# Spreading the preparation of operands over more steps of a two-MLP attention kernel

## The chip, the cores and the metric

The kernel runs on one core of a Trainium2 chip. The metric is device time in microseconds (us): the median of three runs before the change is 1218.3 (1217.76 to 1219.68).

## The reference

Attention runs twice per batch and head: 32 packed queries attend to 576 keys, and then the 576 queries attend to the 32 packed results. Its output, 4608 tokens of 512 features, goes through a first MLP (512 to 2048 to 512, squared ReLU) and a second one (512 to 1024 to 512, with a softmax gate and a layer norm between its two products):

```python
p_packed = sm_attn(p, k, v)                 # B=8, H=8, S=576, D=64, 32 packed rows
x = sm_attn(q, p_packed, p_packed)          # -> [4608, 512]
h = np.maximum(x @ w_in, 0.0)               # first MLP
y = h * h @ w_out
h = y @ w_in2                               # second MLP
solu = h * softmax(h)
ln = (solu - mean(solu)) / np.sqrt(var(solu) + 1e-06) * g_ln
out = ln @ w_out2
```

All of it is float32. A product is made of three TensorE products of rounded parts: each operand x is held as a high half (x rounded to the type fp32r) and a low half (x minus the high half), and high times high, high times low and low times high are added.

## The kernel before, in words

**Steps.** The first MLP runs as 256 steps (variable `i` in the loop at the end of `build`): eight batches, two halves of 288 tokens, 16 slices of 128 hidden features. In step i, `h1` issues six matmuls into a PSUM bank (the names h, ah, al, slot), ScalarE writes the ReLU (rg), ScalarE or GpSimd by turns the square, ScalarE the high half of the square and VectorE the low half (both in the tile ghl); the low half has its place in VectorE's order after the work listed for step i + 1 (`lows`). `ymm`, called three steps later (LAG), issues twelve matmuls of ghl with the weights woh and wol into four accumulators Y. After 16 slices Y is copied out, two copies by ScalarE and two by VectorE, into ys, which goes to y_d in DRAM; the accumulators are used again by the next Y product. These copies come with steps 162, 178, 194, 210, 226 and 242. The start of a step is taken below as the start of ScalarE's ReLU, which is its first operation.

**Work beside the steps.** `at_step(i, fn)` puts a function on step i's list, and it runs when the loop comes to that step. From step 138 (`R0`) to 245 the program order of VectorE, ScalarE and GpSimd is the order written by these lists (`strict`); SyncE's DMAs, and the matmuls of `mm`, are always in that order. Elsewhere a planner orders the instructions by their expected times. On these lists stand the second attention of batches 5 to 7 (`s2_jobs`: that of batch 6 spreads over steps 163 to 185, of batch 7 over 195 to 217), the loads of the first-layer operands (`load_slot`), and the two preparations that the change is about:

- `decode_at` (line 521): 16 units of the second MLP's weights, one every `PD` = 5 steps from step 138. A unit loads 512 KB (raw), and four to six steps later ScalarE and VectorE turn its 64-bit floats into 32-bit ones (dw): one ScalarE operation, one shift and two other operations on VectorE. The first eight units belong to the first weight, the others to the second. After units 3 and 7, and after units 9, 11, 13 and 15, `quads` (line 635) combines four blocks into the seven operands of Strassen's scheme over the next six steps: seven high halves by ScalarE, seven low halves (op) and four differences (dw) by VectorE, each operand stored to wi_d or wx_d.
- `pre_y` (line 753): 14 pairs of 128-token blocks of y, one every `RD` = 6 steps from step 138. A pair loads 512 KB (yf) and makes seven operands of it in steps 4 to 8 after the load: ScalarE writes the high halves, GpSimd the differences and five low halves, VectorE two low halves (yo). Each operand is stored to yc_d two steps after it is made, from one of seven buffers.

**Into the second MLP.** At step `t0` = 230 the memory of both preparations is given up and the pools w2 and y01 take its place. The operands of the first two pairs (`fetch_y`, seven loads of 256 KB each) are loaded at steps 234 and 240, the 14 operand tiles of the first weight (`load_wi`, 512 KB each) at steps 231 to 244, one a step, in the order of the list `WO`; those of the second weight (`load_wx`, 28 of 256 KB) at steps 244 to 257, two a step, into the tiles of the first MLP's second weight as its last products free them. `h2(0)`, the first product of the second MLP for one pair (seven Strassen products of six matmuls), its softmax and layer norm stand at step 249. After the loop come 18 rounds of `h2`, the transposes `tr` and the last product `ou`, ordered by the planner.

`strassen` (line 830) uses its right-hand operands in this order:

```python
p1 = prod("11", "11"); prod("12", "21"); prod("S2", "T2"); prod("S3", "T3")
prod("S1", "T1"); prod("S4", "22"); prod("22", "T4")
```

Of the kernel before, what the change touches and what calls it, by code (L numbers as in the profile page):

```python
# [27 lines left out]
NPRE = 14  # L28
# [4 lines left out]
def f(ap):  # L33
    return ap.bitcast(F32)


def build(tc, qT, kT, vP, pT, w_in, w_out, w_in2, w_out2, g_ln, out):
# [25 lines left out]
    def dma(out, in_):  # L63
        pin(SP.dma_start(out=out, in_=in_))
# [19 lines left out]
    def bank(name):  # L84
        return ps.tile([P, 512], F32, tag="a", name=name, bufs=4)
# [432 lines left out]
    def at_step(i, fn):  # L518
        jobs.setdefault(i if i == "first" else T0 + i, []).append(fn)

    def decode_at(i, mk):
        d = {}
        at_step(i, lambda: d.setdefault("u", mk()))
        for j in range(3):
            at_step(i + 4 + j, lambda: d["u"].step())
# [24 lines left out]
    for b in range(2, B):  # L550
# [9 lines left out]
        for s in range(8):  # L560
            i = 16 + 2 * s + 3
            if b == 2:
                i = (17, 19, 21, 23, 25, 31, 33, 35)[s]
            if b == 4:
                i = max(i, 9 + 24 * s // 5)
# [25 lines left out]
    def load_wi(i):  # L591
        k, o = divmod(i, 7)
        t = W2["p"].tile([P, 2, 512], F32R, name=f"wi{k}{WO[o]}")
        dma(f(t.rearrange("p a c -> p (a c)")), wi_d[k, o])
        wi.setdefault(k, {})[WO[o]] = t
# [7 lines left out]
    WO = ("11", "T1", "22", "21", "T3", "T2", "T4")  # L603
# [9 lines left out]
    def wi_unit(k, q):  # L613
        r0, c0 = (k + 2 * (q // 2)) * P, (q % 2) * 1024

        def fin(wf):
            wq[q] = wf[:, 0]
            if q == 3:
                quads(wi_d[k], 512, *(wq[i] for i in range(4)))

        return Decode(W2["d"], w_in2[r0:r0 + P, c0:c0 + 1024], (1, 512), fin, bufs=(2, 1, 6))

    def wx_unit(k, half):
        q = k + 4 * half

        def fin(wf):
            A.activation(wf[:, 0], wf[:, 0], AF.Copy, scale=W2["g"][:, q:q + 1])
            for i in range(2):
                wq[2 * half + i] = wf[:, 0, i * 256:(i + 1) * 256]
            if half:  # L630
                quads(wx_d[k], 256, *(wq[i] for i in range(4)))

        return Decode(W2["d"], w_out2[q * P:(q + 1) * P], (1, 512), fin, bufs=(2, 1, 6))
# [54 lines left out]
    for n in range(8):  # L688
        i = P1 + 1 + PS * n
# [7 lines left out]
        unit_at(P2 + 1 + u * 12 // 5, 1, u // 2, u % 2, lambda: X["p"], (3, 2, 2))  # L697
    p1 = P2 + 1 + 36 + 9
    at_step(p1, open_prep)
    PD = 5  # L700
    for u in range(16):
        mk = (lambda u=u: wi_unit(u // 4, u % 4)) if u < 8 else (lambda u=u: wx_unit((u - 8) // 2, u % 2))
        decode_at(p1 + 1 + PD * u, mk)
    t0 = 230
    assert p1 + 1 + PD * 15 + 6 <= t0
    at_step(t0, lambda: W2["dst"].close())
    at_step(t0, lambda: X["yst"].close())
# [9 lines left out]
    def halves(t):  # L717
        return [t[:, x * 256:(x + 1) * 256].rearrange("p (a c) -> p a c", a=2) for x in range(2)]


    def operands(q, put, eng):
        a11, a12, a21, a22 = q["11"], q["12"], q["21"], q["22"]
        los = []

        def comb(out, x, y, op=ALU.subtract):
            eng("c").tensor_tensor(out=out, in0=x, in1=y, op=op)

        def split(n, x):
            hi, lo, done = put(n)
            A.copy(hi, x)  # L730

            def go():
                eng(n).tensor_tensor(out=lo, in0=x, in1=f(hi), op=ALU.subtract)  # L733
                done()
            los.append(go)

        def low():
            for fn in los:
                fn()
            los.clear()  # L740

        return [[(split, "11", a11), (split, "12", a12), (split, "22", a22), (comb, a21, a21, a22, ALU.add)], [(low,)],
                [(split, "S1", a21), (comb, a11, a21, a11), (comb, a12, a12, a11), (comb, a22, a22, a11)],
                [(low,), (split, "S2", a11), (split, "S4", a12), (split, "S3", a22)], [(low,)]]

    def quadrants(yl, yr):
        return {"11": yl[:, :, :P], "12": yr[:, :, :P], "21": yl[:, :, P:], "22": yr[:, :, P:]}


    R0, RD = 138, 6  # L750
    assert R0 + RD * (NPRE - 1) >= 213 > R0 + 5 * RD >= 101

    def pre_y(m):
        i0 = R0 + RD * m
# [36 lines left out]
    def places(i):  # L791
        c = {}
        for j, n in enumerate(AO):
            if i < 2:
                if i == 0 and j < 4:
                    t = atp.tile([P, S], F32R, tag=f"a{'hl'[j % 2]}{j // 2}", name="y0", bufs=2)[:, :512]
                else:
                    t = W2["y"].tile([P, 512], F32R, name=f"y{i}{n}")
            elif j < 4:
                if j % 2 == 0:  # L800
                    u = big4(1, [P, 2, 512], "y2", F32R)
                t = u[:, j % 2]
            else:
                t = t25("1" if j == 4 else "2", "y2", F32R)[:, :512]
            c[n] = t
        return c

    def fetch_y(i):
        m = ORDER[i]
        c = places(i)  # L810
        if m < NPRE:
            for j, n in enumerate(AO):
                dma(f(c[n]), yc_d[m][:, j])
            ytl[i] = {n: halves(t) for n, t in c.items()}
            return
        ytl[i] = {n: halves(t) for n, t in c.items()}
        y2 = [p2.tile([P, 2, 256], F32, tag=f"yf{k}", name="yf", bufs=1) for k in range(2)]
        for k in range(2):
            dma(y2[k], y_d[:, 2 * k:2 * k + 2, m * 256:(m + 1) * 256])
        for js in operands(quadrants(*y2), lambda n: (*ytl[i][n], lambda: None), lambda n: V if n in ("22", "12") else G):  # L820
            for fn, *x in js:
                fn(*x)
# [34 lines left out]
    def h2(m):  # L857
        c = ytl.pop(m)
        if m == 0:
            e = big.tile([P, 2, 512], F32, tag="big", name="e", bufs=4)  # L860
        t = [big.tile([P, 2, 512], F32, tag="big", name="hs", bufs=4) for _ in range(2)]
        mx = {}

        def fin(i, o, x, y):
            n = W2["p"].tile([P, 1], F32, tag=f"mx{i}", name="mx", bufs=2)
            V.tensor_tensor_reduce(out=o, in0=x, in1=y, scale=1.0, scalar=mx.get(i, -3.4028234663852886e38), op0=ALU.add, op1=ALU.max,  # L866
                                   accum_out=n)
            mx[i] = n

        strassen(lambda l, k: (c[l][0][:, k], c[l][1][:, k]), wi, 2, 512, (lambda: bank("h")) if m == 0 else (lambda: psh.tile([P, 512], F32, tag="h", name="h", bufs=3)),  # L870
                 t[0][:, 0], t[0][:, 1], t[1][:, 0], t[1][:, 1], vadd, fin)
        hs[m] = t
        for i, h in enumerate(t):
            nm = W2["p"].tile([P, 1], F32, tag="nm", name="nm2", bufs=2)
            V.tensor_scalar_mul(nm, mx[i], -1.0)
            if m:
                e = p2.tile([P, 2, 512], F32, tag="e", name="e", bufs=1)
            sm = W2["p"].tile([P, 1], F32, tag="sm", name="sm3", bufs=2)
            A.activation(e, h, AF.Exp, bias=nm, accum_out=sm)  # L879
            V.tensor_scalar_add(sm, sm, 1e-9)  # L880
            V.reciprocal(sm, sm)
            V.scalar_tensor_tensor(out=h, in0=e, scalar=sm, in1=h, op0=ALU.mult, op1=ALU.mult)  # L882
            st = W2["p"].tile([P, 2, 6], F32, tag="st", name="st", bufs=1)
            for n in range(2):
                V.bn_stats(out=st[:, n, :], in_=h[:, n, :])  # L885
            mv = W2["p"].tile([P, 2], F32, tag="mv", name="mv", bufs=2)
            V.bn_aggr(out=mv, in_=st)
            rstd = W2["p"].tile([P, 1], F32, tag="rstd", name="rstd", bufs=2)
            V.tensor_scalar_add(rstd, mv[:, 1:2], 1e-6)
            G.tensor_tensor(out=rstd, in0=rstd, in1=mhalf, op=ALU.pow)  # L890
            if next(TURN["LNA"]) == "V":
                V.tensor_scalar(out=h, in0=h, scalar1=mv[:, 0:1], scalar2=rstd, op0=ALU.subtract, op1=ALU.mult)  # L892
            else:
                nb = W2["p"].tile([P, 1], F32, tag="nb", name="nb", bufs=1)
                V.scalar_tensor_tensor(out=nb, in0=mv[:, 0:1], scalar=-1.0, in1=rstd, op0=ALU.mult, op1=ALU.mult)
                A.activation(h, h, AF.Identity, bias=nb, scale=rstd)  # L896
# [2 lines left out]
        W2["yst"].close()  # L899

    for i in range(2):
        at_step(t0 + 4 + 6 * i, lambda i=i: fetch_y(i))
    for i in range(14):
        at_step(t0 + 1 + i, lambda i=i: load_wi(i))
    at_step(249, lambda: h2(0))


    K0 = Pack(0, era, False)
# [23 lines left out]
    for t in range(max(max(j for j in jobs if j != "first"), T0 + N + LAG - 1) + 2):  # L932
        i = t - T0
# [196 lines left out]
```

## Time and profile before

| what | us |
|---|---|
| median of three runs | 1218.3 |
| the profiled execution | 1216.89 |
| its span, first to last instruction | 1215.1 |
| TensorE matmuls busy | 1148.2 (94%) |
| VectorE busy | 879.2 (72%) |
| ScalarE busy | 665.6 (55%) |
| GpSimd busy | 581.8 (48%) |

The mean granted TensorE clock is 0.983 of full speed. In the rows below, L58 and L53 are helpers (`mm` and `Engine`) through which most instructions are issued, so instructions are told apart by their tiles: `Y<-ghl,woh` is a Y product, `op<-dw` a combination of weights, `yo<-yf` an operand of y. PE is TensorE, DVE VectorE, ACT ScalarE, POOL GpSimd, SP SyncE. What stands in square brackets behind an instruction is the idle time of its engine just before it, and what ended that.

### The profile page before, as it was taken

The numbers are of one execution on the slowest core, as the hardware profiler recorded it, in microseconds if no ns is written. First come the engines' busy times: TensorE is split into PE (matmuls) and PEld (weight loads), VectorE is DVE, ScalarE is ACT, GpSimd is POOL, SyncE is SP. The second block draws the span as 40 slices with busy tenths as digits, with TensorE's granted clock in tenths as the row PEclk, the third lists the DMA queues.
The fourth block names the chain that finished last, engine by engine and source line by source line (L and its number), as shares of the span: only waits on it lengthen the run. The fifth ranks groups of instructions, "written<-read, shape, count | busy, mean of one in ns | idle before, by whom it ended". The sixth has DMA issues, their size and how long they took to land. (4 is left out here: it accounts for less than half of the span.)

```text
span 1215.1 us, 24017 instructions
## 1 busy us (share of the span) xinstructions
PE 1148.2 (94%) x8652; PEld 1055.3 (87%) x8652; DVE 879.2 (72%) x1700; ACT 665.6 (55%) x1505; POOL 581.8 (48%) x591
## 2 busy tenths in 40 slices
PE   6678899999999999999998899999999999999998
PEld 3368899898999998998998899998889899889897
DVE  4787588745326766579877982257989789889886
ACT  3476555344445555566666674435554655655553
POOL 1112254534225544487866781113654764745743
PEclk9988899999999999999999999999999999999999
DMA  9667697655155899789699799653142143223201
GB/s 331 217 198 193 187 300 225 227 203 199 57 198 155 214 290 303 203 308 378 228 393 340 255 368 366 223 171 114 44 144 90 38 143 105 87 83 109 79 23 48
DMA packets 124775, 238.04 MB, mean 196 GB/s; under 512 B 16624, under 2 KB 44272, under 8 KB 124656
## 3 DMA queue, kind: packets, MB, share of 16 engines
q1 hardware_dynamic: 124656, 236.50, 58.4%
q8 instruction: 68, 1.11, 0.4%
q14 instruction: 51, 0.42, 0.1%
HBM read 144.71 MB, written 91.75 MB: 195 GB/s over the span
## 5 line engine op out<-in xcount | busy, mean ns | idle before, releaser
L58 PE MATMUL Y<-ghl,woh 128*128 128x288 f32 x2048 | 467.6, 304 | 13.5 <-DVE ghl L53 6.5
L58 PEld LDWEIGHTS Y<-ghl,woh 128*128 128x128 f32 x2048 | 348.4, 191 | 28.0 <-DVE ghl L53 7.5
L58 PE MATMUL Y<-ghl,wol 128*128 128x288 f32 x1024 | 305.9, 299 | 0.0
L58 PE MATMUL h<-ah,slot 128*128 128x288 f32 x1024 | 215.7, 299 | 18.4 <-ACT ah L432 10.1
L838 PE MATMUL o<-wx,ch 128*128 128x256 f32 x1008 | 191.3, 287 | 5.3 <-DVE ys L855 2.9
L58 PEld LDWEIGHTS Y<-ghl,wol 128*128 128x128 f32 x1024 | 196.1, 192 | 0.0
L1034 POOL TENSOR_TENSOR cl<-raw,ch 128x512 fp32r<-128x512 f32 x100 | 148.4, 1505 | 96.9 <-ACT ch L1033 51.7
L58 PEld LDWEIGHTS h<-ah,slot 128*128 128x128 f32 x1024 | 167.3, 191 | 21.1 <-ACT ah L432 10.5
L469 POOL TENSOR_TENSOR rg<-rg 128x288 f32<-128x288 f32 x128 | 94.0, 736 | 171.7 <-ACT rg L462 157.6
L838 PEld LDWEIGHTS o<-wx,ch 128*128 128x128 f32 x1008 | 160.0, 192 | 12.2 <-DVE ys L855 4.4
L58 PE MATMUL h<-al,slot 128*128 128x288 f32 x512 | 152.3, 297 | 1.5 <-DVE al L67 1.4
L838 PE MATMUL o<-wx,cl 128*128 128x256 f32 x504 | 142.7, 286 | 2.5 <-POOL cl L1034 2.0
L67 DVE TENSOR_TENSOR ghl<-rg,ghl 128x288 fp32r<-128x288 f32 x149 | 79.5, 539 | 81.7 <-POOL rg L469 60.8
L462 ACT ACTIVATE rg<-h 128x288 f32<-128x288 f32 x148 | 60.7, 410 | 105.8 <-PE h L58 105.3
L53 DVE TENSOR_TENSOR ghl<-rg,ghl 128x288 fp32r<-128x288 f32 x107 | 78.0, 742 | 50.5 <-ACT ghl L53 25.3
L1033 ACT CAST ch<-raw 128x512 fp32r<-128x512 f32 x126 | 76.7, 622 | 62.2 <-DVE raw L1039 54.3
L838 PEld LDWEIGHTS o<-wx,cl 128*128 128x128 f32 x504 | 95.9, 191 | 4.9 <-POOL cl L1034 3.0
L58 PEld LDWEIGHTS h<-al,slot 128*128 128x128 f32 x512 | 97.6, 191 | 2.0 <-DVE al L67 2.0
L67 POOL TENSOR_TENSOR ws<-dw,ws 128x512 fp32r<-128x512 f32 x32 | 42.1, 1314 | 109.0 <-ACT ws L298 81.8
L53 ACT ACTIVATE rg<-h 128x288 f32<-128x288 f32 x108 | 44.1, 409 | 88.2 <-PE h L58 85.0
L838 PE MATMUL h<-wi,y 128*128 128x512 f32 x312 | 83.4, 402 | 0.4 <-DVE hs L855 0.3
L1039 DVE TENSOR_TENSOR raw<-raw 128x512 f32<-128x512 f32 x70 | 73.6, 1060 | 9.9 <-POOL cl L1034 5.0
(170 smaller groups left out, 2125.8 us busy)
## 6 DMA issues: line engine op xcount, KB each, us to landing
pw_d<-pws SPq DMA_DIRECT2D x124, 256.0 KB, 4.4
slot<-pw_d SPq DMA_DIRECT2D x62, 512.0 KB, 6.2
yc_d<-yo SPq DMA_DIRECT2D x98, 256.0 KB, 6.2
y<-yc_d SPq DMA_DIRECT2D x92, 256.0 KB, 4.2
raw<-w_in SPq DMA_DIRECT2D x40, 512.0 KB, 6.4
raw<-w_out SPq DMA_DIRECT2D x24, 512.0 KB, 6.2
kf<-kT SPq DMA_DIRECT2D x32, 288.0 KB, 6.2
out<-ys SPq DMA_DIRECT2D x72, 128.0 KB, 1.7
```

Source lines behind the costliest of these rows:

```text
L53: return (lambda *a, **k: pin(fn(*a, **k))) if strict[0] else fn
L58: pin(PE.matmul(*a, **k))
L67: eng.tensor_tensor(out=lo, in0=x, in1=f(hi), op=ALU.subtract)
L462: A.activation(r, pb[:, :HF], AF.Relu)
L469: G.tensor_tensor(out=gg, in0=r, in1=r, op=ALU.mult)
L838: PE.matmul(bk, x, w[:, y], start=(i == 0), stop=(i == 3 * nk - 1))
L1033: A.copy(c[n][0], x)
L1034: eng.tensor_tensor(out=c[n][1], in0=x, in1=f(c[n][0]), op=ALU.subtract)
L1039: eng.tensor_tensor(out=out, in0=x, in1=y, op=op)
```

## The change

`PD` goes from 5 to 6 and `RD` from 6 to 7: the last unit of weights starts at step 228 and ends with its combinations at step 240, and the last pair of y starts at step 229 and stores at step 239. `t0` moves to 241. The loads of y stand at steps 241 and 247, those of wi at 242 to 248, two a step, and both halves of an operand together, in the order in which `strassen` uses them. `h2(0)` moves from step 249 to 252. `load_wx`, R0, the bursts' own six steps and the ordered stretch (138 to 245) stay.

```diff
-    PD = 5
+    PD = 6
...
-    t0 = 230
+    t0 = 241
...
-    R0, RD = 138, 6
-    assert R0 + RD * (NPRE - 1) >= 213 > R0 + 5 * RD >= 101
+    R0, RD = 138, 7
...
     for i in range(2):
-        at_step(t0 + 4 + 6 * i, lambda i=i: fetch_y(i))
+        at_step(t0 + 6 * i, lambda i=i: fetch_y(i))
     for i in range(14):
-        at_step(t0 + 1 + i, lambda i=i: load_wi(i))
-    at_step(249, lambda: h2(0))
+        o = WO.index(("11", "21", "T2", "T3", "T1", "22", "T4")[i // 2])
+        at_step(t0 + 1 + i // 2, lambda i=i, o=o: load_wi(i % 2 * 7 + o))
+    at_step(252, lambda: h2(0))
```

## Rows read from the trace of the kernel before

**Rows 1.** TensorE's waits, 499 to 732 us: who for whom, us, times, longest.
```profile
PE Y L58 <- DVE ghl L53: 6.5, 4, 2.7
PE Y L58 <- DVE ys L53: 2.6, 2, 2.3
PE h L58 <- DVE t L53: 1.0, 1, 1.0
PE Y L58 <- ACT ghl L53: 0.5, 1, 0.5
```

**Rows 2.** Stretches: us, each engine's busy us (instructions), granted clock, DMA share, GB/s.
```profile
499.30:732.50 233.20, 222.56 (x1619) 217.18 (x1618) 195.46 (x276) 152.77 (x413) 172.71 (x193) 0.99 0.88 316
...
610.00:660.00 50.00, 44.86 (x314) 42.33 (x314) 39.21 (x61) 31.61 (x84) 31.75 (x38) 0.97 1.04 395
...
732.00:787.00 55.00, 55.00 (x414) 55.00 (x413) 12.19 (x27) 24.34 (x60) 8.68 (x13) 1.00 0.79 294
```

**Rows 3.** VectorE's groups, 499 to 732.5 us: busy us, mean ns, idle before.
```profile
L53 DVE TENSOR_TENSOR ghl<-rg,ghl 128x288 fp32r<-128x288 f32 x88 | 69.4, 804 | 18.9 <-POOL rg L53 9.6 <-ACT ghl L53 9.3
L53 DVE SCALAR_TENSOR_TENSOR dw<-raw,dw 128x512 uint32<-128x512 uint32 x32 | 33.4, 1044 | 1.1
L53 DVE TENSOR_TENSOR yo<-yf,yo 128x256 fp32r<-128x256 f32 x28 | 20.2, 723 | 12.5 <-ACT yo L53 12.4
L53 DVE TENSOR_TENSOR op<-dw,op 128x256 fp32r<-128x256 f32 x28 | 18.7, 712 | 0.0
L53 DVE TENSOR_TENSOR op<-dw,op 128x512 fp32r<-128x512 f32 x14 | 11.5, 868 | 0.0
L53 DVE TENSOR_TENSOR dw<-dw 128x256 f32<-128x256 f32 x16 | 11.1, 692 | 0.3
L53 DVE TENSOR_SCALAR dw<-dw 128x512 uint32<-128x512 uint32 x16 | 10.8, 677 | 4.3 <-ACT dw L53 4.1
L53 DVE TENSOR_TENSOR dw<-dw 128x512 f32<-128x512 f32 x8 | 7.8, 979 | 0.1
```

**Rows 4.** ScalarE in time order: first operation of steps 226 and 248.
```profile
732.45 0.41 ACT L53 ACTIVATE rg<-h 128x288 f32<-128x288 f32 x1 [1.25 <-PE h L58]
...
785.27 0.41 ACT L462 ACTIVATE rg<-h 128x288 f32<-128x288 f32 x1 [1.59 <-PE h L58]
```

**Rows 5.** TensorE in time order: the end of its longest wait.
```profile
642.56 0.53 PE L58 MATMUL Y<-ghl,woh 128*128 128x288 f32 x2 [2.68 <-DVE ghl L53]
```

**Rows 6.** Stretches: two of low clock, and the loads of operands.
```profile
643.50:646.90 3.40, 3.40 (x16) 3.40 (x16) 3.33 (x5) 2.26 (x7) 3.06 (x3) 0.50 1.05 374
694.70:698.10 3.40, 3.10 (x13) 3.10 (x14) 3.33 (x8) 0.75 (x2) 1.16 (x2) 0.50 0.61 208
740.90:765.60 24.70, 24.70 (x188) 24.70 (x187) 4.95 (x11) 10.23 (x25) 3.33 (x5) 1.00 0.96 373
```

**Rows 7.** ScalarE's waits, 610 to 660 us.
```profile
ACT yo L53 <- DMA yc_d<-yo: 4.9, 5, 3.8
```

**Rows 8.** SyncE's issues in time order, steps 226 to 249.
```profile
737.57 0.32 SPq L64 DMA_DIRECT2D wi<-wi_d  x1
...
738.88 2.07 SPq L64 DMA_DIRECT2D y<-yc_d  x4
...
772.86 0.56 SPq L64 DMA_DIRECT2D y_d<-ys  x1
...
777.16 10.45 SPq L64 DMA_DIRECT2D wx<-wx_d  x10
```

**Rows 9.** TensorE in time order: the second MLP's first pair.
```profile
787.42 2.97 PE L838 MATMUL h<-wi,y 128*128 128x512 f32 x12
...
796.44 0.85 PE L838 MATMUL h<-wi1T,y 128*128 128x512 f32 x3
```

**Rows 10.** End of the first pair's normalization; first transposes of it.
```profile
807.85 1.23 ACT L896 ACTIVATE hs<-hs,nb,rstd 128x1024 f32<-128x1024 f32 x1
...
822.12 1.03 PE L1029 MATMUL ct<-ident,hs 128*128 128x128 f32 x8
```

## The prediction

> **What bounds the kernel now.** I read the 40 slices of the profile first: TensorE is busy nine tenths or more nearly everywhere between 60 and 1190 us, so only its idle time and its low clock can be won back, and the question is where they lie around the change. I looked second at who TensorE waited for between 499 and 732 us, the stretch in which the operands of y and the second MLP's weights are prepared. Four rows hold all of it: 6.5 + 2.6 + 1.0 + 0.5 = 10.6 us, nearly all on VectorE [rows 1]. Third, the table by stretch: in 233.2 us VectorE was busy 195.5; from 610 to 660 TensorE lost 5.1 us while the DMA share was 1.04 at 395 GB/s; and from 732 to 787, where the preparation is over, TensorE lost nothing and VectorE worked 12.2 of 55 us [rows 2]. So an overfull stretch lies ahead of an almost empty one. That there is no fourth culprit shows in the waits themselves: the longest, 2.68 us, is a second-layer product (Y) waiting for ghl, the low half that VectorE writes for each step [rows 5].
>
> A step takes (785.27 - 732.45) / 22 = 2.40 us when nothing waits [rows 4]. This is the supply: 2.40 us of VectorE in a step.
>
> **The change, part by part.**
>
> *Slower pace: the load.* No instruction is added or removed. Sixteen weight units cost VectorE 33.4 + 10.8 = 44.2 us, 2.76 each. The combinations behind them (seven operands, made after every fourth unit of the first weight and after every second one of the other) cost (11.5 + 7.8) / 2 = 9.65 us for each of two big sets and (18.7 + 11.1) / 4 = 7.45 for each of four small ones. The 14 pairs of y cost 20.2, 1.44 each. What no edit touches is ghl, 69.4 / 88 = 0.79 us a step, and the other 195.5 - 69.4 - 113.5 = 12.6 us, 0.14 a step [rows 2, 3]. ScalarE (152.8 us) and GpSimd (172.7) get the same relief, but were behind in few places, so VectorE carries the sum.
>
> The later weights, one small set in two units: before, ten steps supply 24.0 us, and 7.45 + 2 x 2.76 + 10/6 x 1.44 + 9.3 = 24.7 are asked, 103%. After, twelve steps supply 28.8 and 7.45 + 5.52 + 12/7 x 1.44 + 11.2 = 26.6 are asked, 92%. The earlier weights, one big set in four units: 44.1 of 48.0 us before (92%), 47.9 of 57.6 after (83%). So before, VectorE can't get rid of a backlog from about step 180 on; after, it can.
>
> *Slower pace: what stays.* The combinations still come as a burst of six steps (14.4 us). After the change a big burst asks 9.65 + 2.76 + 6/7 x 1.44 + 5.6 = 19.2, which leaves VectorE 4.8 us behind; a small one 17.0, 2.6 behind. How much lag is free? ghl of step i has its turn with step i+1 and is wanted when the first-layer products of step i+3 end: two steps, 4.8 us, less some 1.8 us for the work queued with it, so about 3 us. Each of the two big bursts (steps 162 to 168 and 186 to 192) then still costs 4.8 - 3.0 = 1.8 us. A small burst costs nothing by itself, but the copies out of Y every 16 steps (steps 162, 178, 194, 210, 226) must be done before the next Y product, with only the 0.8 us of six first-layer products (a third of a step's 18) as slack; at 226 one falls late in a burst: 2.6 - 0.8 = 1.8 us. Left: 1.8 + 1.8 + 1.8 = 5.4 us; gone: 10.6 - 5.4 = **5.2 us**. From below, the whole 10.6 could go; from above, 1.6 if the bursts queue as now.
>
> *Stores of y.* The yo tiles are seven, one pair's worth, so a pair's operands wait for the stores of the pair before. From 610 to 660 ScalarE waited for them five times, 4.9 us, once 3.8 [rows 7], and this delayed ghl. One step more between pairs gives 2.4 us of that 3.8 back, and the remaining 1.4 is inside the free lag. This is part of the 5.2.
>
> *Clock.* The granted clock was 0.50 (1.2 GHz) for 3.40 us at 643.5, right behind the 2.68 us wait, and for 3.40 us again at 694.7, in the 2.3 us wait for ys [rows 1, 5, 6]. Of 3.40 us at half rate 1.7 are lost, 3.4 in both. The shorter waits of the stretch brought no fall. With none expected over about 1.8 us I count both as gone: **3.4 us**; bounds 0 and 3.4.
>
> *Loads moved to steps 241 to 248.* Fourteen wi loads of 512 KB, fourteen y loads of 256 KB, one y_d store of 576 KB and the first ten wx loads of 256 KB that SyncE's order puts between them are 7.34 + 3.67 + 0.59 + 2.62 = 14.2 MB. Before, the first load left at 737.57, seven us ahead of step 231 (732.45 + 5 x 2.40), and all but the last two wi had been issued before 772.86 [rows 8]; now everything begins with step 241, since the last stores of the preparation end only then. The first pair's h2 takes (796.44 + 0.85) - 787.42 = 9.9 us, 1.4 a product [rows 9]; begun at step 252, 11 x 2.40 = 26.4 us after step 241, it wants the last product's weights at 26.4 + 6 x 1.4 = 34.8. At 395 GB/s [rows 2] the 14.2 MB take 36.0 us, 1.2 us late; at 373, the mean of the loads before [rows 6], 38.1 us, 3.3 late; begun a step earlier, nothing. The order of use is what makes this bearable: the first six products' weights are there. I take **+1.2 us**, bounds 0 and +3.3. SyncE's queue is in order, and behind these loads stand only the rest of wx, which already had to wait for the Y products of steps 240 and on (777.16, ten issues in 10.45 us [rows 8]) and which the second layer's first use, after h2 of the second pair, doesn't feel.
>
> *h2 of the first pair three steps later.* It costs TensorE the same. Its cover on the other side shrinks: the normalization ends at 807.85 + 1.23 = 809.1, 11.8 us after h2, and its transposes came at 822.1 [rows 10], 24.8 after; three steps (7.2 us) fewer leave 17.6. Still 5.8 to spare, so 0. If that cover went, DVE and ScalarE work of up to 6 us would stand in the open.
>
> *Sum.* -5.2 - 3.4 + 1.2 = -7.4 us. Against the profiled execution (1216.89 us, span 1215.1) that is 1209.5; the median of the runs, 1218.3, lies 1.4 above that execution, so as a median **1210.9 us**.
>
> **The rivals.**
>
> *All of it goes (0.10).* The lag never exceeds 3 us, and the loads are in time: -10.6 - 3.4 = -14.0, 1204.3. For it speaks the mean load of 83 to 92%; against it, that two bursts and a Y copy still meet.
>
> *The backlog moves with the bursts (0.20).* A burst is as dense as ever, the attention of the seventh batch (from step 163) now lies wholly on the burst of step 162, and the stores of the second big set move into the steps whose DMA share was already 1.04 [rows 2]. Then 9.0 us of waits and one fall of the clock stay: -1.6 - 1.7 + 1.2 = -2.1, 1216.2. Against it: the weights' stretch as a whole drops below 100%.
>
> *Loads too late (0.08), the slower case.* h2 stands in front of TensorE without weights. If the transfers reach only the 294 GB/s of 732 to 787 [rows 2], 14.2 MB need 48.3 us, 13.5 late; with one fall of the clock behind it the sum is -5.2 - 3.4 + 13.5 + 1.7 = +6.6, 1224.9. It decides the sign for the measurement from a lateness of 9.3 us, that is under 323 GB/s. Against it: two rows, mixed traffic and the very same loads, show 395 and 373, and the planner may set Y products ahead of h2.
> The Trainium skill ("DMA: Bandwidth & Descriptors", section "Where 436 GB/s comes from") speaks for lateness: between HBM and SBUF it puts the limit per core at about 358 GB/s. By that, an estimate, the 14.2 MB would take 39.7 us, 4.9 late, and the sum would be -3.7, 1214.6 as a median. The 395 GB/s over 50 us of mixed loads and stores [rows 2] lies above that limit, so I keep the row's rate.
>
> **How the numbers follow.** The forecast has 0.62, its own range 1207 to 1214 (bounds of the loads, one fall of the clock, one to two us of the last stage, which the planner orders anew). The range of 8 in 10 is 1206 to 1218: it takes in the second rival and most of the way to the first. About 0.2% (2.4 us) can be told from no change: faster means under 1215.9. That holds for nearly all of the forecast, the first rival and a quarter of the second: 0.75. Same: 0.17. Slower: 0.08.
>
> **What would show it.** Between the starts of steps 138 and 226 TensorE's waits should fall from 10.6 to about 5 us, on ghl near steps 166 and 190 and on ys near 226; ScalarE's waits for yc_d should nearly vanish; the clock should show no 0.50 there. VectorE should be busy until about step 240 instead of 228. In front of the first pair's last product a wait of at most 3 us on wi would be right; one above 5 us, or a gain with the waits unchanged, would prove the working wrong.

## The result, and the profile after

The changed kernel takes 1203.3 us (median of four runs, 1202.19 to 1206.03) against 1218.0 (1217.61 to 1219.68): ratio 0.9885 [0.9866, 0.9905]. It is faster, as forecast, but by 14.7 us instead of 7.4, and lies below the low end of the range (1206). The profiled execution took 1202.19 us, its span is 1200.4.

Here is where the span went, cut at the starts of steps 138, 226 and 248 (ScalarE's ReLU). The waits are TensorE's between steps 138 and 240; "falls" are stretches of 3.4 us at a granted clock of 0.50 in those steps. The last five columns are runs of the section on the experiments: the same kernel again (e1, e12), and three kernels with parts of the change.

| us | before | after | e1 | e12 | weights only | y only | loads only |
|---|---|---|---|---|---|---|---|
| start of step 138 | 499.3 | 496.3 | 497.8 | 496.6 | 501.8 | 499.7 | 499.5 |
| steps 138 to 226 | 233.1 | 222.1 | 221.8 | 222.2 | 223.7 | 225.8 | 233.6 |
| steps 226 to 248 | 52.8 | 53.6 | 53.4 | 53.6 | 52.8 | 53.0 | 53.2 |
| step 248 to the end | 429.8 | 428.3 | 430.5 | 429.1 | 429.7 | 429.2 | 430.1 |
| waits | 10.6 | 2.7 | 2.7 | 2.7 | 3.7 | 6.5 | 10.5 |
| falls | 2 | 0 | 0 | 0 | 0 | 0 | 2 |

The second line is the change's own: 11.0 us. The lines outside it make another 3.7 us of the first result, and that part doesn't repeat in full (e1: 0.3, e12: 2.6).

TensorE's waits of the changed kernel from 496 to 752 us, which is up to step 240, show which of [rows 1] are left (columns as there):

```profile
PE Y L58 <- DVE ghl L53: 1.6, 2, 1.4
PE Y L58 <- ACT ys L53: 0.6, 2, 0.3
PE h L58 <- DVE t L53: 0.3, 1, 0.3
PE Y L58 <- DVE ys L53: 0.2, 1, 0.2
```

Of 6.5 us for ghl 1.6 are left, of 2.6 for VectorE's copies out of Y 0.2. The next rows are the table by stretch of the changed kernel, as in [rows 2]: steps 138 to 226, a part of it with full DMA, steps 226 to 248, and the loads of the second MLP's operands.

```profile
496.35:718.47 222.12, 219.60 (x1618) 214.54 (x1617) 175.09 (x253) 143.36 (x385) 152.99 (x176) 1.00 0.83 298
611.00:633.00 22.00, 21.95 (x164) 21.71 (x163) 20.20 (x26) 16.59 (x43) 15.55 (x18) 1.00 1.04 409
718.47:772.11 53.64, 53.37 (x398) 53.14 (x397) 29.43 (x49) 31.47 (x86) 23.50 (x29) 1.00 0.84 307
755.00:773.20 18.20, 18.20 (x137) 18.20 (x136) 4.03 (x9) 8.52 (x21) 3.27 (x5) 1.00 1.03 393
```

VectorE is busy 175 of 222 us (79%) where it was 195 of 233 (84%), and the difference stands in the next stretch, 29.4 us of work where there were 12.2. The granted clock is 1.00 throughout; both falls of [rows 6] are gone. From 611 to 633 us, the second big burst, the DMA share is 1.04 as it was, VectorE works 20.2 of 22 us, and TensorE loses nothing. Three groups of VectorE show that the work is the same and only spread: from 496 to 718 us there are 28 of the long operations on dw and 24 yo, where [rows 3] had 32 and 28.

```profile
L53 DVE TENSOR_TENSOR ghl<-rg,ghl 128x288 fp32r<-128x288 f32 x88 | 67.7, 784 | 19.9 <-ACT ghl L53 10.3 <-POOL rg L53 9.5
L53 DVE SCALAR_TENSOR_TENSOR dw<-raw,dw 128x512 uint32<-128x512 uint32 x28 | 26.9, 959 | 1.0
L53 DVE TENSOR_TENSOR yo<-yf,yo 128x256 fp32r<-128x256 f32 x24 | 17.0, 708 | 13.0 <-ACT yo L53 13.0
```

SyncE's issues in time order: the loads of y, of wi, the y_d store between them, and the last two operands of wi.

```profile
752.25 1.91 SPq L64 DMA_DIRECT2D y<-yc_d  x4
...
755.62 2.40 SPq L64 DMA_DIRECT2D wi<-wi_d  x2
759.63 0.56 SPq L64 DMA_DIRECT2D y_d<-ys  x1
...
783.97 0.32 SPq L64 DMA_DIRECT2D wi1T<-wi_d  x1
```

And TensorE and ScalarE in time order around h2 of the first pair: its first product, its last two parts, the next Y product, the end of its normalization and the first transposes.

```profile
781.55 1.81 PE L837 MATMUL h<-wi,y 128*128 128x512 f32 x7
...
790.46 0.93 PE L837 MATMUL h<-wi0T,y 128*128 128x512 f32 x3 [0.37 <-DMA wi0T<-wi_d]
791.61 0.97 PE L837 MATMUL h<-wi1T,y 128*128 128x512 f32 x3 [0.22 <-DMA wi1T<-wi_d]
792.42 0.29 PE L58 MATMUL Y<-ghl,woh 128*128 128x288 f32 x1
...
802.30 1.24 ACT L895 ACTIVATE hs<-hs,nb,rstd 128x1024 f32<-128x1024 f32 x1 [2.06 <-DVE nb L894]
...
810.22 1.03 PE L1029 MATMUL ct<-ident,hs 128*128 128x128 f32 x8
```

The last operand is late by 0.37 + 0.22 = 0.59 us, and between the end of the normalization (803.54) and its first transposes 6.7 us are left.

### The profile page after: what moved, and what is told of

Read it like the earlier page. It is cut to its first block, busy times and chain, and to the rows that moved or that the text cites. A ratio compares the mean times of both kernels' runs of the same rounds, so it can differ in the third digit from the quotient of the medians.

```text
span 1200.4 us, 24027 instructions
## 1 busy us (share of the span) xinstructions
PE 1143.6 (95%) x8652; PEld 1049.9 (87%) x8652; DVE 875.2 (73%) x1700; ACT 664.1 (55%) x1505; POOL 578.6 (48%) x591
## 5 line engine op out<-in xcount | busy, mean ns | idle before, releaser
L58 PEld LDWEIGHTS h<-ah,slot 128*128 128x128 f32 x1024 | 166.4, 190 | 20.0 <-ACT ah L432 10.5
L837 PEld LDWEIGHTS o<-wx,ch 128*128 128x128 f32 x1008 | 158.9, 190 | 12.1 <-DVE ys L854 4.2
```

The lines of the kernel that those rows point to most:

```text
L58: pin(PE.matmul(*a, **k))
L837: PE.matmul(bk, x, w[:, y], start=(i == 0), stop=(i == 3 * nk - 1))
```

## The experiments

**The change again**, twice, unchanged (e1_change_again and e12_change_third), to see how much of the 14.7 us repeats.

> The changed kernel once more. Theory (pace): the gain is the waits and clock falls between the starts of steps 138 and 226, 11 us; the 3 us that the profile gained before step 138, where both kernels have the same instructions in the same order, are chance of single executions. Then steps 138 to 226 take 222 us again within 1 us, the start of step 138 lies anywhere from 495 to 500 us, and five rounds give a ratio of 0.989 to 0.992. Rival (whole program): something of the changed program makes its start faster too; step 138 starts at 496 to 497 again and the ratio stays at 0.988.

> The changed kernel, to stand beside the next two on one chip. Steps 138 to 226 take 222 us within 1 us; ratio 0.989 to 0.992.

Measured: ratios 0.9904 [0.9890, 0.9918] and 0.9901 [0.9883, 0.9918], 11.7 and 12.1 us of the time before. The stretch of steps 138 to 226 repeats within 0.4 us. What doesn't repeat lies ahead of step 138 and behind step 248, where the clock falls in different places from profile to profile. The kernel before has a fall at 227 us, worth 1.7 us, that no profile of the change has. Ten of the fourteen profiles have it (at 224 to 230 us), among them kernels with the change (e7 and e13, below); the change and the loads alone don't. Behind step 248, before has one fall, at 1193 us, and the three profiles of the change have none, two and one. The rest of the front's 3.0 us I can't place: over the eleven profiles whose instructions up to there are the same, step 138 starts between 496.3 and 501.8 us. I take 12 us as the change's size, and 11 as that which the traces explain.

**The parts alone.** From the changed kernel, (e2_weights_only) the pace of y put back, (e3_y_only) the pace of the weights put back, (e4_loads_only) both:

```diff
-    R0, RD = 138, 7
+    R0, RD = 138, 6     # e2, e4
-    PD = 6
+    PD = 5              # e3, e4
```

> Weights at six steps a unit, y back at six steps a pair; loads as changed. Theory (VectorE overfull): a small set of combinations in twelve steps asks 27.0 of 28.8 us, 94%, so waits between steps 138 and 226 fall from 10.6 to 3 to 4 us with no clock fall or one; ratio 0.990 to 0.993. Rival (stores of y hold ScalarE): the pace of y matters; ScalarE's waits for yc_d stay at 5 us or more, TensorE's waits stay above 6 us, ratio 0.995 or more.

> y at seven steps a pair, weights back at five steps a unit; loads as changed. Theory (VectorE overfull): 24.3 of 24.0 us are asked in the later weights' ten steps, 101%, so 7 to 10 us of waits and one or two clock falls stay; ratio 0.996 to 0.999. Rival (stores of y): the wait of 2.7 us and its clock fall go, ScalarE's waits for yc_d vanish, waits are 6 us or less, ratio 0.993 to 0.995.

> Both paces as before; only the later memory change (step 241), the order and places of the loads and h2 at step 252 stay. Theory (pace): waits of 9 to 12 us and two clock falls between steps 138 and 226 as before, under 1 us of waits for weights in the first h2; ratio 0.999 to 1.001. Rival (whole program): the last stage or the start gains 2 to 3 us by itself, ratio 0.997 to 0.998.

Measured: 0.9923 [0.9908, 0.9939], 0.9947 [0.9928, 0.9966] and 0.9997 [0.9982, 1.0011]. The move of the loads, of h2 and of the memory costs nothing that can be measured. The slower weights alone bring 9.4 us in the stretch and the slower y alone 7.3, both together 11.0: they share what they remove. Each ends both falls of the clock (3.4 us); in waits they bring 6.9, 4.1 and together 7.9. TensorE's waits in steps 138 to 226, first with the weights alone:

```profile
PE Y L58 <- DVE ghl L53: 1.8, 4, 0.5
PE h L58 <- DVE t L53: 1.1, 1, 1.1
PE Y L58 <- ACT ys L53: 0.8, 2, 0.6
```

then with y alone:

```profile
PE Y L58 <- ACT ys L53: 2.8, 1, 2.8
PE Y L58 <- DVE ghl L53: 1.8, 2, 0.9
PE Y L58 <- DVE ys L53: 1.0, 2, 0.7
```

Slower y cures ghl as well as slower weights do (6.5 to 1.8 us in both), and leaves one late copy out of Y, of ScalarE. It brings more than I expected of it (0.996 to 0.999), and it takes more out of the stretch than VectorE's four yo operations: GpSimd is busy 156.0 us there instead of the 172.7 of [rows 2], ScalarE 148.3 instead of 152.8, and VectorE's 88 low halves take 62.6 us instead of the 69.4 of [rows 3].

The load that I had worked out for the later weights (103% before, 101% with y alone) was not there either. From step 180 to 226 VectorE worked 109.0 us in the kernel before, and 46 steps of 2.40 us give 110.4: 99%. With y alone it is 95%, with the weights alone 94%, with both 90%. So VectorE was full rather than overfull, with next to no time left to make up for the 12.4 us in which it waited for ScalarE's yo [rows 3].

The rival of these runs, the stores of y that hold ScalarE, does not explain the gain, though the ratio with y alone lies in its range. ScalarE's waits for yc_d between steps 138 and 240 are 6.5 us before, 5.1 with the weights alone and 4.2 with y alone, while TensorE's waits fall from 10.6 to 3.7 and 6.5.

The run with y alone settles something on the clock. TensorE in time order there, its longest wait, and the stretch behind it:

```profile
646.70 0.40 PE L58 MATMUL Y<-ghl,woh 128*128 128x288 f32 x1 [2.80 <-ACT ys L53]
```

```profile
646.70:650.10 3.40, 3.28 (x22) 2.61 (x22) 3.40 (x8) 1.97 (x6) 1.89 (x4) 1.00 1.02 384
```

A wait of 2.80 us, longer than the 2.68 of [rows 5], was followed by a granted clock of 1.00. So the length of one wait doesn't decide whether the clock falls.

**How much lag is free?** The step that failed, as will be seen. One step less between the two layers, in the changed kernel (e5_lag2):

```diff
-    LAG = 3
+    LAG = 2
```

> The changed kernel with Y products two steps behind the first-layer products instead of three (the loads of wx, tied to it, move one step forward). Theory (free lag): a low half is ready 1.7 us after its step begins when VectorE is not behind, so with three steps VectorE may lag 5.5 us, with two 3.1. That was the figure in the prediction, and most bursts then show: waits between steps 138 and 240 of 8 to 13 us instead of 2.7, some clock falls, ratio to before 0.997 to 1.003. Rival (mean load): it is enough that VectorE's mean load is under 100%; waits stay under 5 us, ratio 0.990 to 0.993.

Measured: 1.0067 [1.0047, 1.0087], slower than forecast by more than the bound. TensorE's waits in steps 138 to 226:

```profile
PE Y L58 <- DVE ghl L53: 12.1, 13, 1.9
```

Thirteen waits, all for ghl, in place of two; to step 240 there are 13.1 us. The clock never fell there. The lag is what hides the bursts, and one step of it is worth some 10 us of waits. The rest of the slowdown lies outside the stretch; LAG holds for every step from 48 on, but what it costs there was not traced.

**One step more**, in the kernel before (e8_before_lag4) and in the changed one (e9_after_lag4): `LAG = 4` and nothing else.

> The kernel before with Y products four steps behind (the loads of wx one step later). Theory (overfull and free lag): 2.4 us more of lag hide part of the 7.0 us of waits on ghl, not the 3.6 on copies out of Y and on transposes, and the backlog past step 180 still grows; waits of 5 to 8 us, ratio 0.995 to 0.999. Rival (bursts alone, no overfull stretch): all waits on ghl vanish, waits of 4 us or less, no clock fall, ratio 0.991 to 0.994.

> The changed kernel with Y products four steps behind. Theory (free lag): the waits on ghl (1.7 us in the stretch) vanish, those on the copies out of Y and on transposes (1.1) stay; ratio to before 0.988 to 0.990, 1 to 2 us under the change. Rival (four ghl buffers are too few for four steps): ScalarE waits for TensorE to free ghl, and the time is that of the change or up to 3 us longer.

Measured: 1.0087 [1.0072, 1.0101] and 0.9961 [0.9946, 0.9976], against some 0.990 of the change. TensorE's waits of the kernel before with lag 4, in steps 138 to 226:

```profile
PE Y L58 <- ACT ys L53: 4.1, 3, 3.2
PE Y L58 <- DVE ys L53: 3.4, 3, 1.7
PE Y L58 <- DVE ghl L53: 2.6, 1, 2.6
PE Y L58 <- ACT ghl L53: 1.4, 1, 1.4
```

The waits for ghl shrink from 7.0 to 4.0 us, but those for the copies out of Y grow from 2.6 to 7.5. No theory had this right. In the changed kernel the last waits for ghl do go (none is left, the stretch takes 220.7 us instead of 222.1), but step 138 starts 7.4 us later and the time behind step 248 is 5.2 us longer, so that the forecast of 1 to 2 us less missed by some 7 us.

Neither run is a clean test of more lag. The tile ghl has four buffers, and with four steps ScalarE waits for Y products to free one: in steps 138 to 226 for 27.8 us (37 times) in the kernel before and 34.2 us (42 times) in the changed one, where with three steps it never does. This is the condition of the rival in the second expectation. In the quiet step 231 of the changed kernel the low half then ends 2.55 us after its step began instead of 1.71, and 6.8 us are free up to its Y product instead of 5.3: the fourth step bought 1.5 us, not 2.4. How much of the late copies, and of the time lost elsewhere, comes from the buffers is open.

**The order of the loads** put back to that of the list, twice (e7_order_undone, e13_order_again):

```diff
-        at_step(t0 + 1 + i // 2, lambda i=i, o=o: load_wi(i % 2 * 7 + o))
+        at_step(t0 + 1 + i // 2, lambda i=i, o=o: load_wi(i))
```

> The changed kernel with the loads of wi in the old order (all seven of the first half, then all of the second), still two a step. Theory (order of use carries the loads): the eleventh and thirteenth tiles land at about 786.5 and 790.3 us and are wanted by the second and third product at 783 and 788; TensorE waits 5 to 7 us in the first h2, ratio 0.995 to 0.997. Rival (planner): the planner sorts the matmuls of h2 by expected arrival, so that TensorE waits under 1 us and the ratio is that of the change, 0.990 to 0.992.

> The changed kernel with the loads of wi in the old order, once more, beside the change. Its profile showed 1.3 us of waits in the first h2 against 0.6, but its ratio was 0.994 on another chip. Theory (planner): the order is worth under 1 us; ratio within 0.001 of the change beside it, 0.990 to 0.992. Rival (order of use): something that the one profile did not show costs 3 to 4 us; ratio 0.993 to 0.995 with the change beside it at 0.990.

Measured: 0.9942 [0.9927, 0.9956] and 0.9922 [0.9907, 0.9937], each about 0.2 to 0.4% above the change's own. So neither expectation had the time right. But h2 hardly feels the order: TensorE waits in it for weights 0.4 us in both, against 0.6, 0.2 and 0.8 in the three profiles of the change, and with the waits for VectorE 1.3 and 1.2 us against 0.6, 1.2 and 0.8. In these kernels the planner sets the matmuls of h2 in the order in which it expects the operands. Most of the difference in time stands ahead of step 138, which starts at 500.1 and 501.0 us against 496.3 to 497.8, though the instructions up to there stand in the same order on every engine; 1.7 us of it are the fall of the clock at 227 us. Why is open; it isn't the loads, which come a hundred steps later.

**h2 put back to step 249** in the changed kernel (e10_h2_249):

```diff
-    at_step(252, lambda: h2(0))
+    at_step(249, lambda: h2(0))
```

> The changed kernel with the first h2 back at step 249. The tiles of the last two products landed at 787.8 and 791.6 us, and from 774.3 on they would be wanted at 781.3 and 789. Theory (loads set the place of h2): TensorE waits 6 to 10 us in the first h2, perhaps with a clock fall of 1.7 us, ratio 0.996 to 1.000. Rival (the loads have slack): waits under 2 us, ratio 0.989 to 0.992.

Measured: 0.9975 [0.9963, 0.9987]; step 248 to the end took 440.2 us. TensorE's waits from 775 to 812 us, and the stretch of low clock:

```profile
PE h L837 <- issue: 6.0, 1, 6.0
PE h L837 <- DVE nm L874: 1.0, 1, 1.0
```

```profile
789.90:800.10 10.20, 8.19 (x22) 6.05 (x23) 4.51 (x12) 1.24 (x2) 0.00 (x0) 0.50 0.59 227
```

The profile names no releaser ("issue"), but the product that waits, the last but one of h2, began at 790.9, and the loads of its two operands are this row of SyncE's issues; the first of the two landed at 790.83:

```profile
785.20 0.97 SPq L64 DMA_DIRECT2D wi<-wi_d  x2
```

So it waited for the first of them. The wait has the size forecast; the fall of the clock, which began within it at 789.9, was three times as long as the ones in [rows 6], 10.2 us, worth 5.1. The two make 11 us, and 440.2 is 12 above the 428.3 of the change (the medians, 1214.9 and e12's 1205.0, are 9.9 apart). The loads do set the place of h2, and the three steps are what makes them free.

**Taking VectorE's share of yo away** in the kernel before: all low halves to GpSimd (e11_before_yo_gpsimd), which leaves the pace as it was and relieves VectorE of 20.2 us.

```diff
-    operands(q, put, lambda n: V if n in ("22", "S3") else G)
+    operands(q, put, lambda n: G)
```

> The kernel before at its old pace, with the two low halves of y that VectorE makes per pair given to GpSimd. Theory (VectorE overfull): ten steps of the later weights then ask 22.3 of 24.0 us, 93%; waits between steps 138 and 226 fall from 10.6 to 4 to 7 us, ratio 0.993 to 0.997. Rival (GpSimd): its 172.7 us of 233 become 200, its squares come late and ghl with them; waits of 10 us or more, ratio 0.999 or more.

Measured: 0.9991 [0.9976, 1.0006], waits of 9.9 us instead of 10.6, and one fall of the clock, at 603.5. (The profile is of the fastest of the twelve executions, 1211.89 us; their median is 1216.47.) My theory missed. The stretch of steps 138 to 226 in this kernel, and VectorE's groups in it:

```profile
497.30:729.10 231.80, 221.90 (x1618) 215.73 (x1618) 189.36 (x248) 153.27 (x413) 196.60 (x221) 0.99 0.88 317
```

```profile
L53 DVE TENSOR_TENSOR ghl<-rg,ghl 128x288 fp32r<-128x288 f32 x88 | 72.7, 848 | 37.2 <-POOL rg L53 25.2 <-ACT ghl L53 4.6 <-PE Y L58 2.8
L53 DVE SCALAR_TENSOR_TENSOR dw<-raw,dw 128x512 uint32<-128x512 uint32 x32 | 35.8, 1118 | 1.1
L53 DVE TENSOR_TENSOR op<-dw,op 128x512 fp32r<-128x512 f32 x14 | 13.2, 983 | 0.0
```

VectorE's busy time fell by 6.1 us, not by 20.2: each group of [rows 3] that is left took longer for one operation (ghl 848 ns against 804, the operation on raw 1118 against 1044, op 983 against 868). And it waited 25.2 us for GpSimd's squares (rg), 9.6 before, since GpSimd was now 85% busy. Work can't be pushed from the one to the other here; a slower pace relieves both.

## Why the prediction was wrong in size

The mechanism was right in outline: a full stretch ahead of an almost empty one, nothing added, and most waits on VectorE gone with both falls of the clock. Of the 7.3 us between the 7.4 forecast and the 14.7 measured, 3.6 lie in steps 138 to 226 (11.0 us gained there), and 3.7 lie outside them, for which the prediction had no term and of which the repeats show 0.3 and 2.6. By its steps:

**The failed step: "How much lag is free?", answered with "about 3 us".** I took it that ghl of a step has its turn with the next step's work, that is one step late and 1.8 us behind that. In a quiet step the trace after shows otherwise. Step 231 in time order: its ReLU, its low half, and the Y product that takes it.

```profile
730.93 0.41 ACT L53 ACTIVATE rg<-h 128x288 f32<-128x288 f32 x1 [1.46 <-PE h L58]
...
732.18 0.46 DVE L53 TENSOR_TENSOR ghl<-rg,ghl 128x288 fp32r<-128x288 f32 x1 [1.95 <-ACT ghl L53]
...
737.96 0.30 PE L58 MATMUL Y<-ghl,woh 128*128 128x288 f32 x1
```

The low half ends at 732.64, 1.7 us after its step began, and its Y product begins at 737.96: 5.3 us are free (5.6 up to the product's third matmul, at 738.23, the first to use the low half). The trace before shows the same 1.7 and 5.3 us in step 231, so this could have been read ahead of the prediction. A place in VectorE's order ties it to no step of TensorE; when VectorE has nothing to do, it runs ahead. Step 191, in the second big burst, shows how far that goes:

```profile
628.52 0.41 ACT L53 ACTIVATE rg<-h 128x288 f32<-128x288 f32 x1 [0.43 <-PE h L58]
...
635.17 1.90 DVE L53 TENSOR_TENSOR ghl<-rg,ghl 128x288 fp32r<-128x288 f32 x2
...
636.21 0.53 PE L58 MATMUL Y<-ghl,woh 128*128 128x288 f32 x2 [0.28 <-DVE ghl L53]
```

Its low half, the first of the two in the row, ends about 636.2, 7.6 us after the step began and 5.9 later than in the quiet step, and costs TensorE 0.28 us. The 4.8 us by which I had put VectorE behind in a big burst were not far off; with 5.3 us free they cost nothing, and the sum's own terms would have been left with 1.8, gone 8.8, and 1218.3 - 8.8 - 3.4 + 1.2 = 1207.3. That these terms make the 11.0 us of the stretch is in part luck: 7.9 us of waits went, not 8.8, and the loads cost less. Lag 2 is the counter-test: it takes 2.4 of the 5.3 us, leaves the 3 I had counted with (2.9 in its step 231), and 13.1 us of waits came. So with 3 us free my count of 5.4 would in turn have been too low, for one burst then makes several waits (at 666.1 and 669.8 us, for instance). Both errors lie in the same term and partly cancel.

**Waits left: 5.4 forecast, 2.7 measured.** Neither big burst costs more than 0.3; nor does the copy out of Y at step 226, which I had at 1.8: it waited 0.27, on ScalarE. The one wait over 0.4 us, 1.37 on ghl at 659.6, is in a small burst that I had said costs nothing; the last batch's attention, from step 195 on, lies on it, which my count gave an average of 0.14 us a step. That the attention makes this wait was not tested.

**Clock: -3.4 forecast, both falls gone in all three profiles of the change.** My reason (no fall under some 1.8 us of wait) was weaker than the result: a fall came behind 1.90 us (e11, at 603.5) and none behind 1.92 (lag 2) or 2.80 (y alone). What holds is the comparison of kernels, not the bound.

**Loads: +1.2 forecast (0 to 3.3), 0.59 measured, and nothing in the timed run of the loads alone.** h2 came 26.5 us after step 241, forecast 26.4; the transfers ran at 393 GB/s while the loads had the engines, 395 assumed. There is luck in the term too: the first load left 2.8 us ahead of the start of step 241 (752.25 against 755.06), and the last weights landed at 791.57, 39.3 us later and not 36.0. The claim that the order of use makes this bearable fell: without it h2 waits no longer for its weights (0.4 us).

**Stores of y: right in the outcome, not in the reason.** ScalarE waits for yc_d nowhere in the profile after, 6.5 us in the stretch before (4.9 of them in [rows 7]). But the step more between pairs, which was to give 2.4 us of the longest wait back, doesn't do it by itself: with y alone, seven steps apart, a wait of 3.8 us is still there.

**h2 three steps later: right.** 6.7 us of cover are left, 5.8 forecast.

**VectorE busy until step 240: right**, by the 29.4 us in steps 226 to 248.

Of the rivals, "all of it goes" was nearest in the number (1204.3), with a chance of 0.10, and that is luck: its condition, a lag of at most 3 us, did not hold (5.9 us in step 191), 2.7 of its 10.6 us of waits stayed, and 3.7 us came from outside the stretch. The backlog did not move with the bursts, and the loads were late by 0.6 us alone. The range's low end was 1206; the repeats have medians of 1205.2 and 1205.0. Down to the first rival it would have held these two, not the first result.
The 358 GB/s per core of the Trainium skill ("DMA: Bandwidth & Descriptors", section "Where 436 GB/s comes from") were no limit here: the table above has 409 over 22 us.

Open is why step 138 starts 1.5 to 3 us earlier in the three profiles of the change and not in kernels that differ from it only behind step 240, and with it why the fall of the clock at 227 us is missing in those three.

## What to carry to other kernels

Read the free lag of an in-order engine from a quiet stretch of the trace, as producer's end to consumer's start, before counting what a burst costs; the program's order alone makes it look shorter than it is. When a stretch is full and the next one is almost empty, slow the pace of the background work. Here that was better than one step more of lag, for which ghl had too few buffers, and than shifting work to a second engine that slows the first down. And don't add up what two such changes bring alone: here 9.4 and 7.3 us made 11.0.

## What the runs showed of the hardware

An operation of VectorE on two tensors can take twice as long while GpSimd works. VectorE's low half takes 0.46 us at 732.18 (above), while GpSimd stands idle from 729.74 to 733.89, and 0.99 us here; VectorE and GpSimd of the changed kernel in time order:

```profile
741.82 0.92 POOL L53 TENSOR_TENSOR yo<-yf,yo 128x256 fp32r<-128x256 f32 x1
```

```profile
742.07 0.99 DVE L53 TENSOR_TENSOR ghl<-rg,ghl 128x288 fp32r<-128x288 f32 x1
```

GpSimd's operation ends at 742.74, VectorE's, begun 0.25 us behind it, at 743.06: it ends as if most of it had waited for the other. In steps 138 to 226 of the kernel before, the 24 low halves that met no operation of GpSimd took 0.40 to 0.46 us, 0.45 in the mean; the 64 that met one took 0.94 in the mean and up to 1.42. With all of yo on GpSimd (85% busy instead of 74%) 72 of the 88 met one, and the mean of the low halves rose from 804 to 848 ns, and the rest with it: hence the 6.1 us that VectorE got back of 20.2. The share alone doesn't set the mean (784 ns in the changed kernel and 727 with y alone, both with GpSimd 69% busy); it counts which operations meet.
The Trainium skill ("SBUF — State Buffer", section "Who interferes with whom") says that an operation of VectorE on two tensors, both in SBUF, contends with GpSimd's reads, and that the ports which the two engines share are an exclusive lock. The rows agree with the contention, and nearly with the lock: 0.32 us lie between the two ends, where VectorE's operation takes 0.46 alone.

The clock's fall in the 6.0 us wait of e10 lasted 10.2 us, three times as long as those of [rows 6], behind waits of 2.68 and 2.3 us.
